# Decode attention: the first key block in one load, and TensorE starts when all of it has landed

## The chip, the cores and the metric

The kernel runs on one core of one Trainium2 chip. A core has TensorE (PE, with its weight loads shown as PEld), VectorE (DVE), ScalarE (ACT), GpSimd (POOL) and SyncE (SP). Each takes its instructions in program order, and they wait for each other through semaphores. Sixteen DMA engines move data between HBM and the on-chip memory. The metric is the device time of one execution in microseconds, the median of several runs.

## What is computed

One decoding step of grouped-query attention over a long cache, mixed by a gate with a small token-mixing network. The cache is nearly all of the data: 8 key/value heads of 65536 positions with 256 numbers each, in bfloat16, once for keys and once for values, 537 MB together.

```python
# x: [1, 1, 448]; k_cache, v_cache: [1, 8, 65536, 256]; wq: [448, 4096]; wo: [4096, 448]
q = (x @ wq).reshape(1, 1, 16, 256).transpose(0, 2, 1, 3)
k = repeat(k_cache, 2, axis=1); v = repeat(v_cache, 2, axis=1)
p = softmax(einsum("bhqd,bhkd->bhqk", q, k) * 256 ** -0.5)
a = einsum("bhqk,bhkd->bhqd", p, v).transpose(0, 2, 1, 3).reshape(1, 1, 4096) @ wo
h = layernorm(x)
b = (gelu(h[..., None] * w1 + b1) @ w2 + b2)        # a small network on each number of h
g = sigmoid((x * gate_w).sum())
out = g * a + (1 - g) * b
```

## The kernel before

**Blocks and chunks.** The keys are taken in `NP` = 32 blocks, four to a head, and the values likewise. A block is 16384 positions: `NV` = 128 slots of 128 positions by 256 numbers, 8.4 MB, 64 KB in each of 128 partitions. A block has `BODY` = 8 chunks of `NT` = 16 slots. `HV` = 64 slots are half a block, four chunks (`DC` = 4).

**The key ring.** `kring` has room for one and a half blocks, `NV + HV` slots. Blocks with an even number stand in slots 0 to 127, those with an odd number in slots 64 to 191. So the middle 64 slots are shared by each block and the next. TensorE takes the middle slots first (`tiles(HV)`, chunks 0 to 3), then the half that is a block's own (`tiles(0)` or `tiles(NV)`, chunks 4 to 7). Once chunks 0 to 3 are transposed the next block may be loaded. `vbuf` has room for one block of values; a new one may be loaded when TensorE has used the old one. At the start `vbuf` also holds the query weights `wq` and the small inputs.

**The order of loads.** All large loads are issued by SP in its program order, on one queue: `wo` for the first head, `wq`, key block 0 in two halves (L268 and L269), value block 0, key block 1, value block 1, key block 2, and so on. Ahead of each stands its wait: value block 0 waits for the query work that reads `vbuf` (`s_q`, `s_hb`), key block j for the transposes of chunk 3 of block j - 1 (`sem_tr`, L290), value block j for the products with value block j - 1 (`sem_pv`, L276). Key blocks 2, 3 and 31 also come in parts, each with semaphores of its own (`sem_kc`, `sem_kq`).

**TensorE's order.** After the query work a loop runs over the blocks. For block 0 and block 1: `keys` (for each chunk 16 transposes L355 into `kst`, which VectorE and ScalarE copy to `ktT` at L675 and L820, and 32 score products L376 one chunk behind), then the maxima (L393, L395) that VectorE turns into the softmax's shift, then `values` (denominators L400, then 128 products with the value block, L407, in pieces of 72, 24, 16 and 16). The last product tells `sem_pv`. From block 2 on the maxima and values of a block come after the keys of the next one.

**The waits around the change.** In `transposes`, chunk 0 of block j waits for `sem_k` to reach 16 (j + 1), and chunk 4 waits for `sem_kb` and, in three blocks, for one of `sem_kc`. The first half to be loaded of block 0, slots 64 to 127, counts on `sem_k`; the second one, slots 0 to 63, on `sem_kb`.

Of the kernel before, what the change touches and what calls it, by code (L numbers as in the profile page):

```python
# [12 lines left out]
def bass_gated_mix__gqa_block_cached__mixer_token_mlp__decode_kernel(  # L13
# [37 lines left out]
    NV = BODY * NT  # L51
# [32 lines left out]
    HV = NV // 2  # L84
# [11 lines left out]
    with ctx:  # L96
        def sb(shape, dt, name):
            return ctx.enter_context(nc.sbuf_tensor(name, shape, dt))
# [4 lines left out]
        def new_sem(name):  # L103
            return ctx.enter_context(nc.semaphore(name))

        kring = sb([P, NV + HV, DH], bf16, "kring")
# [87 lines left out]
        prj = psum([P, 512], f32, "prj")  # L194

        sem_k = new_sem("sem_k")
        sem_kb = new_sem("sem_kb")
        sem_kc = [new_sem("sem_kc%d" % i) for i in range(3)]
        sem_kq = [new_sem("sem_kq%d" % i) for i in range(2)]
        sem_v = new_sem("sem_v")  # L200
# [49 lines left out]
        def src(cache, j, n0=0, n1=NV):  # L250
            g, m = divmod(j, PPH)
            s = cache[0, g, m * BODY * CH:(m + 1) * BODY * CH, :].rearrange("(p n) d -> p n d", p=P)
            return s[:, n0:n1, :].rearrange("p n d -> p (n d)")

        @block.sync
        def _(eng):
            def load_wo(g):
                w = A_wo[g * REP * DH:(g + 1) * REP * DH, :]
                eng.dma_start(wo_rows, w.rearrange("(p i) n -> p (i n)", i=2 * REP)).then_inc(sem_wo, 16)

            load_wo(0)
            eng.dma_start(wq_s.rearrange("p u n -> p (u n)"),
                          A_wq.rearrange("r n -> (r n)").rearrange("(p m) -> p m", p=P)).then_inc(sem_wq, 16)
            def load(dst, cache, j, n0, n1, at, sem):
                eng.dma_start(dst[:, at + n0:at + n1, :].rearrange("p n d -> p (n d)"), src(cache, j, n0, n1)
                              ).then_inc(sem, 16)

            load(kring, A_k_cache, 0, HV, NV, 0, sem_k)  # L268
            load(kring, A_k_cache, 0, 0, HV, 0, sem_kb)  # L269

            def load_v(j):
                if j == 0:
                    eng.wait_ge(s_q, 1)
                    eng.wait_ge(s_hb, 1)
                else:
                    eng.wait_ge(sem_pv, j)  # L276
                load(vbuf, A_v_cache, j, 0, NV, 0, sem_v)
                g, m = divmod(j, PPH)
                if m == 0 and 1 <= g < H - 1:
                    eng.wait_ge(s_proj, g)  # L280
                    load_wo(g)

            for j in range(NP):
                if j == LEAD + 1:
                    eng.wait_ge(sem_tr[NB - 1], BODY * LEAD)
                    load(kring, A_k_cache, j, HV, NV, HV, sem_kc[1])
                    eng.wait_ge(sem_tr[NB - 1], BODY * LEAD + DC // 2)
                    load(kring, A_k_cache, j, 0, HV // 2, HV, sem_kq[0])
                if j >= 1:
                    eng.wait_ge(sem_tr[NB - 1], BODY * (j - 1) + DC)  # L290
                if j == LEAD:
                    load(kring, A_k_cache, j, HV, NV, 0, sem_k)
                    load(kring, A_k_cache, j, 0, HV, 0, sem_kc[0])
                elif j == LEAD + 1:
                    load(kring, A_k_cache, j, HV // 2, HV, HV, sem_kq[1])
                elif j == NP - 1:
                    load(kring, A_k_cache, j, 0, HV, HV, sem_k)
                    load(kring, A_k_cache, j, HV, NV, HV, sem_kc[2])
                elif j >= 1:
                    load(kring, A_k_cache, j, 0, NV, HV * (j % 2), sem_k)  # L300
                if j < LEAD:
                    load_v(j)
                elif j > LEAD:
                    load_v(j - 1)


            for (n0, n1), sem in zip(pieces, sem_vp):
                if n0 == 0:
                    eng.wait_ge(sem_tr[NB - 1], BODY * (NP - 1) + DC)
                elif n0 == NRING:  # L310
                    eng.wait_ge(sem_pv, NP - 1)
                load(kring if n1 <= NRING else vbuf, A_v_cache, NP - 1, n0, n1, 0, sem)
            eng.wait_ge(s_proj, H - 1)
            for h in range(REP):
                w = A_wo[(HQ - REP + h) * DH:(HQ - REP + h + 1) * DH, :]
                eng.dma_start(wo_sb[:, h, :], w.rearrange("(p j) n -> p (j n)", j=2)).then_inc(sem_wl[h], 16)
            eng.wait_ge(s_fin, NCG)
            eng.dma_start(out_ap, out_row[:, :]).then_inc(sem_out, 16)
            eng.wait_ge(sem_out, 16)
# [16 lines left out]
        def _(pe):  # L336
# [3 lines left out]
            def transposes(k, c, j, u16, x2):  # L340
                if k == 0:
                    pe.wait_ge(sem_k, u16)
                if k == DC:
                    pe.wait_ge(sem_kb, 16)
                    for p, sem in zip((LEAD, LEAD + 1, NP - 1), sem_kc):
                        with pe.If(j == p):
                            pe.wait_ge(sem, 16)

                done = pe.snap(c + 1, min_val=1, max_val=NC)

                def tiles(at):
                    for b in range(NB):
                        pe.wait_ge(sem_ev[b], done)
                        for i in range(4):
                            ins = pe.transpose(kst[:, b, i * P:(i + 1) * P],  # L355
                                               kring_f[:, at + NT * (k % DC) + 4 * b + i, :], ident[:, :])
                        ins.then_inc(sem_tr[b], 1)

                if k < DC:
                    tiles(HV)  # L360
                else:
                    with pe.If(x2 == 0):
                        tiles(0)
                    with pe.Else():
                        tiles(NV)
# [16 lines left out]
            def keys(c0, j, *where):  # L382
                j1 = pe.snap(j + 1, min_val=1, max_val=NP)
                transposes(0, c0, j, *where)
                for k in range(1, BODY):
                    transposes(k, c0 + k, j, *where)
                    scores(k - 1, c0 + k - 1, j1)
                scores(BODY - 1, c0 + BODY - 1, j1)
# [43 lines left out]
            def piece_wait(n):  # L432
                for (n0, _), sem in zip(pieces, sem_vp):
                    if n == n0:
                        pe.wait_ge(sem, 16)
# [423 lines left out]
```

## Time and profile before

| | |
|---|---|
| Median of 3 runs | 1264.3 us (1264.19 to 1264.69) |
| The profiled execution | 1264.2 us, span 1262.9 us |
| TensorE busy | 964.6 us, 76% of the span |
| VectorE, ScalarE busy | 500.2 us, 544.5 us |
| Mean granted clock of TensorE | 0.85 |
| DMA | 544.35 MB, mean 431 GB/s |

Times in the profile are counted from the start of the span. SPq is the queue of SP: it issues DMAs and has no busy time of its own. In the page's second part each digit is the busy share of a fortieth of the span, in tenths. In a timeline a row is: start, time taken, engine, line, operation, what it writes and reads, count, and in brackets how long the engine was idle before and what ended that. In the chain of what ended last a DMA row runs from issue to landing, and "issue" is time in which an engine waited for nothing that the profile shows. A DMA lands when the last of its sixteen parts has counted on its semaphore. In windows, the granted clock of TensorE, the DMA share and GB/s are the last three columns; a DMA packet is put down to the window in which it begins, so a share can be over 1.

### The profile page before, as it was taken

Reading aid. Unit: us, or ns where it says so; the run is one execution under the profiler, and the core shown is the slowest. Engines: PE = TensorE matmul, PEld = TensorE weight load, DVE = VectorE, ACT = ScalarE, POOL = GpSimd, SP = SyncE. Lnnn points to the kernel's source line nnn. Section 1 sums busy time; section 2 is a strip of 40 time slices with the busy share of each in tenths; the row PEclk is TensorE's granted clock in tenths of the full one; section 3 lists DMA queues with packets and bytes.
Section 4 is the critical chain, followed back from the end, with each engine's and each line's share of the span. In section 5 each row is a group of like instructions: output and inputs, shape, how many; then the busy total and the mean of one; then the engine's idle time right before and its main releaser. Section 6 shows DMA issues by size and latency. Waiting matters only on the chain.

```text
span 1262.9 us, 39617 instructions
## 1 busy us (share of the span) xinstructions
PE 964.6 (76%) x17024; PEld 881.7 (70%) x17024; DVE 500.2 (40%) x1128; ACT 544.5 (43%) x692; POOL 0.9 (0%) x7
## 2 busy tenths in 40 slices
PE   4768877688777797767878678876679867698786
PEld 3667876678766687666777667776678756687674
DVE  4334434444544435444444433343333423334342
ACT  2444543345533445333554334443344533345451
POOL 0000000000000000000000000000000000000000
PEclk8779887888878888888987879888798878888897
DMA  9999999999999999999999999999999999999998
GB/s 417 431 421 426 449 432 432 430 432 444 432 434 430 434 432 432 432 434 436 436 434 428 439 432 432 432 440 432 434 432 434 428 440 436 434 432 434 423 438 365
DMA packets 12053, 544.35 MB, mean 431 GB/s; under 512 B 1417, under 2 KB 1676, under 8 KB 2828
## 3 DMA queue, kind: packets, MB, share of 16 engines
q1 hardware_dynamic: 11954, 544.22, 99.7%
q8 instruction: 6, 0.10, 0.0%
q10 hardware_dynamic: 90, 0.01, 0.0%
q14 instruction: 3, 0.02, 0.0%
HBM read 544.22 MB, written 0.00 MB: 431 GB/s over the span
## 4 chain that ended last, share of the span: by engine, by line
DMA 60%; PE 36%; issue 2%; DVE 2%; DVEq 0%; ACT 0%; SPq 0%
DMA kring<-in_A_k_cache_dram 57%; PE kst L355 26%; PE sps L376 6%; DMA vbuf<-in_A_v_cache_dram 3%; PE acc L407 3%; PE acc L457 0%; PE prj L468 0%; PE sps L395 0%; DVE ktT L675 0%; DVE accs L709 0%; PE acc L400 0%; ACT z_b L825 0%; PE sps L393 0%; DVE mrow L686 0%; DVE z_b L656 0%
## 5 line engine op out<-in xcount | busy, mean ns | idle before, releaser
L355 PE MATMUL kst<-ident,kring 128*128 128x128 f32 x4096 | 556.9, 296 | 189.5 <-DMA kring<-in_A_k_cache_dram 166.6
L820 ACT ACTIVATE ktT<-kst 128x1024 bf16<-128x1024 bf16 x512 | 498.6, 1021 | 338.7 <-PE kst L355 338.3
L355 PEld LDWEIGHTS kst<-ident,kring 128*128 128x128 f32 x4096 | 505.1, 154 | 198.6 <-issue 192.3
L675 DVE COPY ktT<-kst 128x1024 bf16<-128x1024 bf16 x512 | 353.9, 692 | 436.0 <-PE kst L355 410.4
L376 PEld LDWEIGHTS sps<-qcur,ktT 128*128 128x128 bf16 x8192 | 238.0, 97 | 2.6
L376 PE MATMUL sps<-qcur,ktT 128*128 128x2 bf16 x8192 | 236.6, 163 | 0.0
L407 PE MATMUL acc<-vbuf,pT 128*2 128x256 bf16 x4008 | 160.0, 335 | 6.5 <-DMA vbuf<-in_A_v_cache_dram 3.7
L407 PEld LDWEIGHTS acc<-vbuf,pT 128*2 128x2 bf16 x4008 | 110.8, 102 | 47.6 <-issue 4.4
L803 ACT ACTIVATE fade<-mdif 128x2 f32<-128x2 f32 x32 | 6.5, 203 | 302.1 <-DVE mdif L692 302.1
L686 DVE TENSOR_REDUCE mrow<-sps 2x1 f32<-2x128 f32 x32 | 8.9, 278 | 159.9 <-PE sps L393 159.9
L395 PEld LDWEIGHTS sps<-mdiag,mones 2*128 2x128 f32 x64 | 11.2, 217 | 28.0 <-DVE mdiag L688 28.0
L807 ACT ACTIVATE pT<-sps,mneg 128x64 f32 x128 | 30.4, 335 | 0.0
L395 PE MATMUL sps<-mdiag,mones 2*128 2x2 f32 x64 | 13.9, 285 | 21.3 <-DVE mdiag L688 21.3
L393 PE MATMUL sps<-ident,mcol 128*2 128x128 f32 x32 | 9.0, 282 | 27.3 <-issue 25.8
L825 ACT ACTIVATE z_b<-z_b 128x448 bf16<-128x448 bf16 x14 | 8.1, 576 | 48.1 <-DVE z_b L662 48.1
L400 PE MATMUL acc<-pT,ones_sq 128*128 128x32 bf16 x256 | 12.0, 182 | 21.9 <-issue 18.4
L709 DVE COPY accs<-acc 128x288 f32<-128x288 f32 x8 | 3.7, 458 | 62.4 <-PE acc L407 62.4
L393 PEld LDWEIGHTS sps<-ident,mcol 128*2 128x2 f32 x32 | 2.6, 80 | 36.2 <-issue 28.1
L681 DVE TENSOR_REDUCE mcol<-sps 128x2 f32<-128x256 f32 x32 | 13.5, 423 | 33.8 <-PE sps L376 33.8
L400 PEld LDWEIGHTS acc<-pT,ones_sq 128*128 128x128 bf16 x256 | 8.8, 99 | 26.0 <-issue 22.3
L704 DVE TENSOR_SCALAR acc<-acc,fader 128x256 f32<-128x256 f32 x32 | 15.8, 493 | 2.5
L497 PE MATMUL kst<-vbuf,xcol 128*64 128x512 bf16 x28 | 5.5, 571 | 8.8 <-DMA vbuf<-in_A_wq_dram 8.8
(111 smaller groups left out, 173.9 us busy)
## 6 DMA issues: line engine op xcount, KB each, us to landing
kring<-in_A_k_cache_dram SPq DMA_DIRECT2D x7, 4096.0 KB, 26.4
kring<-in_A_v_cache_dram SPq DMA_DIRECT2D x1, 4608.0 KB, 27.6
kring<-in_A_k_cache_dram SPq DMA_DIRECT2D x2, 2048.0 KB, 15.1
vbuf<-in_A_wq_dram SPq DMA_DIRECT2D x1, 3584.0 KB, 12.0
wo_sb<-in_A_wo_dram SPq DMA_DIRECT2D x7, 448.0 KB, 25.5
vbuf<-in_A_v_cache_dram SPq DMA_DIRECT2D x1, 1536.0 KB, 9.3
vbuf<-in_A_v_cache_dram SPq DMA_DIRECT2D x1, 1024.0 KB, 11.4
vbuf<-in_A_v_cache_dram SPq DMA_DIRECT2D x1, 768.0 KB, 12.8
```

The source lines that it names most:

```text
L355: ins = pe.transpose(kst[:, b, i * P:(i + 1) * P], kring_f[:, at + NT * (k % DC) + 4 * b + i, :], ident[:, :])
L376: ins = pe.matmul(sps[:, 0, 2 * (NT * k + nt):2 * (NT * k + nt) + 2], ktT[:, par, b, ntl * DH + dj:(ntl + 1) * DH:2], qcur[:, dj, :], star ...
L393: pe.transpose(mxT, mcol[:, :], ident[:, :]).then_inc(s_mT, 1)
L395: pe.matmul(mxB, mones[:, :], mdiag[:, :], start=True, stop=True).then_inc(s_mB, 1)
L400: pe.matmul(acc[:, DENC:SELC], ones_sq[:, :], pT[:, r, :], start=False, stop=(r == BODY - 1), skip_group_check=True)
L407: ins = pe.matmul(acc[o:o + REP, 0:DH], pT[:, r, 2 * nt:2 * nt + 2], buf[:, n, :], start=False, stop=False, skip_group_check=True)
L675: vec.tensor_copy(ktT[:, k % KTB, b, :], kst_b[:, b, :]).then_inc(sem_ev[b], 1)
L681: vec.tensor_reduce(out=mcol[:, :], in_=scores_all.rearrange("p (n hh) -> p hh n", hh=REP), axis=AX.X, op=ALU.max)
L686: vec.tensor_reduce(out=mrow[:, :], in_=mxT, axis=AX.X, op=ALU.max)
L704: vec.tensor_scalar(acc[:, 0:DENC], acc[:, 0:DENC], fader[:, :], None, op0=ALU.mult).then_inc(s_acc, 1)
L807: ins = act.activation(pT[:, bass.ds(p0, DC), hh:2 * NT:REP], scores_all.rearrange("p (a r n hh) -> p a hh r n", a=2, r=DC, hh=REP)[:, hal ...
L820: act.activation(ktT[:, k % KTB, b, :], kst_b[:, b, :], AF.Copy).then_inc(sem_ev[b], 1)
```

## The change

Key block 0 is loaded by one DMA of 128 slots that counts on `sem_k`. The semaphore `sem_kb` and the wait for it before chunk 4 are gone. As `sem_k` now reaches 16 only with the whole block, chunk 0 waits for all of it.

```diff
-        sem_kb = new_sem("sem_kb")
...
-            load(kring, A_k_cache, 0, HV, NV, 0, sem_k)
-            load(kring, A_k_cache, 0, 0, HV, 0, sem_kb)
+            load(kring, A_k_cache, 0, 0, NV, 0, sem_k)
...
                 if k == 0:
                     pe.wait_ge(sem_k, u16)
                 if k == DC:
-                    pe.wait_ge(sem_kb, 16)
                     for p, sem in zip((LEAD, LEAD + 1, NP - 1), sem_kc):
```

The kernel after has three lines less, so what stood at L265, L355, L376 and L407 stands at L264, L352, L373 and L404.

SP's first rows before, with their waits. Rows of L265 are the loads of keys and values, and the two sizes a partition's numbers in half a block (16384) and in a whole one (32768); `sem_tr3` is the last of the four `sem_tr`:

```order
L259 DMA wo_sb<-in_A_wo_dram 128x1792
L262 DMA vbuf<-in_A_wq_dram 128x14336
L265 DMA kring<-in_A_k_cache_dram 128x16384 x2
L265 DMA vbuf<-in_A_v_cache_dram 128x32768 [waits s_hb,s_q]
L265 DMA kring<-in_A_k_cache_dram 128x32768 [waits sem_tr3]
L265 DMA vbuf<-in_A_v_cache_dram 128x32768 [waits sem_pv]
```

And after:

```order
L258 DMA wo_sb<-in_A_wo_dram 128x1792
L261 DMA vbuf<-in_A_wq_dram 128x14336
L264 DMA kring<-in_A_k_cache_dram 128x32768
L264 DMA vbuf<-in_A_v_cache_dram 128x32768 [waits s_hb,s_q]
L264 DMA kring<-in_A_k_cache_dram 128x32768 [waits sem_tr3]
L264 DMA vbuf<-in_A_v_cache_dram 128x32768 [waits sem_pv]
```

Two half loads became one whole load at the same place, and the rows behind it stand as they did.

TensorE's rows before chunk 4, before the change. The scores of chunk 2 end here, then come the branches for the blocks that load in parts:

```order
L376 MATMUL sps<-qcur,ktT 128x2 x32
L346 COMPARE_AND_BRANCH [waits sem_kb]
L346 UNCONDITIONAL_BRANCH [waits sem_kc0]
L346 COMPARE_AND_BRANCH
L346 UNCONDITIONAL_BRANCH [waits sem_kc1]
```

And after:

```order
L373 MATMUL sps<-qcur,ktT 128x2 x32
L343 COMPARE_AND_BRANCH
L343 UNCONDITIONAL_BRANCH [waits sem_kc0]
L343 COMPARE_AND_BRANCH
L343 UNCONDITIONAL_BRANCH [waits sem_kc1]
```

Only the wait went; no instruction of TensorE moved.

## The prediction

> **What bounds the kernel now.** I read the page first, then what the loads on the SP queue wait for, then the chain and the timeline of the first 130 us, because the change touches one load near the start.
>
> ```profile
> PE 964.6 (76%) x17024; PEld 881.7 (70%) x17024; DVE 500.2 (40%) x1128; ACT 544.5 (43%) x692; POOL 0.9 (0%) x7
> ...
> DMA  9999999999999999999999999999999999999998
> ...
> q1 hardware_dynamic: 11954, 544.22, 99.7%
> q8 instruction: 6, 0.10, 0.0%
> ```
>
> The SP loads' queue (q1) fills 99.7% of sixteen DMA engines' time, TensorE 76%. The 544 MB set the time, as long as the next load is always queued before the one ahead of it drains. So the one question is whether the change lets the queue run dry, and for how long: a dry microsecond is not made up, since no later slice is idle.
>
> ```profile
> SPq L265 <- PE kst L355: 610.2, 34, 26.9
> SPq L265 <- PE acc L407: 569.0, 30, 28.3
> ```
>
> These are the waits of the SP queue itself. Key loads wait for transposes (L355), value loads for the value products (L407). A late TensorE therefore makes loads late, and the lead of each load over the landing of the one ahead of it is the slack. The issues near the start, and two of the steady part, are these (2.13 and 83.42 are each the second of a pair, shown by a narrower window):
>
> ```profile
> 0.74 0.40 SPq L259 DMA_DIRECT2D wo_sb<-in_A_wo_dram  x1
> ...
> 2.13 0.43 SPq L265 DMA_DIRECT2D kring<-in_A_k_cache_dram  x1
> 21.76 0.33 SPq L265 DMA_DIRECT2D vbuf<-in_A_v_cache_dram  x1
> 34.79 0.33 SPq L265 DMA_DIRECT2D kring<-in_A_k_cache_dram  x1
> 63.44 0.33 SPq L265 DMA_DIRECT2D vbuf<-in_A_v_cache_dram  x1
> 83.05 0.82 SPq L265 DMA_DIRECT2D kring<-in_A_k_cache_dram  x2
> ...
> 83.42 0.45 SPq L265 DMA_DIRECT2D kring<-in_A_k_cache_dram  x1
> ...
> 143.41 0.33 SPq L265 DMA_DIRECT2D kring<-in_A_k_cache_dram  x1
> 162.67 0.33 SPq L265 DMA_DIRECT2D vbuf<-in_A_v_cache_dram  x1
> ```
>
> The time from issue to landing comes last in each row of the list of DMA issues, asked for one issue at a time. In order: the very first load (wo, issued at 0.74), the second half of key block 0 (2.13), value block 0 (21.76), value block 1 (63.44), the two halves of key block 2 (83.05 and 83.42), key block 4 (143.41), value block 3 (162.67).
>
> ```profile
> wo_sb<-in_A_wo_dram SPq DMA_DIRECT2D x1, 448.0 KB, 3.4
> ...
> kring<-in_A_k_cache_dram SPq DMA_DIRECT2D x1, 4096.0 KB, 31.2
> ...
> vbuf<-in_A_v_cache_dram SPq DMA_DIRECT2D x1, 31.4
> ...
> vbuf<-in_A_v_cache_dram SPq DMA_DIRECT2D x1, 28.2
> ...
> kring<-in_A_k_cache_dram SPq DMA_DIRECT2D x1, 4096.0 KB, 18.3
> ...
> kring<-in_A_k_cache_dram SPq DMA_DIRECT2D x1, 4096.0 KB, 27.7
> ...
> kring<-in_A_k_cache_dram SPq DMA_DIRECT2D x1, 25.9
> ...
> vbuf<-in_A_v_cache_dram SPq DMA_DIRECT2D x1, 26.0
> ```
>
> So the second key half lands at 33.3, value block 0 at 53.2 and value block 1 at 91.6. Value block 3 is issued 6.6 us before key block 4 lands (143.4 + 25.9 = 169.3).
>
> The chain that ended last, in its first 75 us, then TensorE's own timeline:
>
> ```profile
> 1.66 21.21 DMA kring<-in_A_k_cache_dram
> 22.87 0.92 issue
> 23.79 5.80 PE kst L355 x32
> ...
> 34.79 37.53 DMA kring<-in_A_k_cache_dram
> 72.32 0.13 issue
> 72.46 5.40 PE kst L355 x32
> ```
>
> ```profile
> 53.18 4.43 PE L407 MATMUL acc<-vbuf,pT 128*2 128x256 bf16 x77 [0.65 <-DMA vbuf<-in_A_v_cache_dram]
> 60.46 2.94 PE L407 MATMUL acc<-vbuf,pT 128*2 128x256 bf16 x51 [2.85 <-issue]
> ```
>
> The first key half lands at 22.87 and TensorE starts at 23.79. The 0.92 is not the load: TensorE was still walking into its loop, since at 72.32 the same wait costs 0.13. Key block 1 lands at 72.32. Value block 1 is issued at 63.44, when the products end at 60.46 + 2.94 = 63.40. Its lead is 72.32 - 63.44 = 8.9 us.
>
> **The change part by part.**
>
> *One load in place of two.* Two halves of a block land 9.7 us apart (83.42 + 27.7 less 83.05 + 18.3, about 9.75). A whole load takes 91.6 - 72.3 = 19.3. Two halves are thus 0.1 to 0.2 us dearer than a whole. SP issues one DMA less at 2.1 us, hidden, as nothing on SP follows before 21.76. The block's landing is the next item's. I count 0 for the transfer; the bounds are -0.2 and 0.
>
> *The wait before chunk 4 goes.* The second half had landed at 33.3, before key block 1's release at 34.79 and chunk 4 behind it. It held nothing up: 0.
>
> *TensorE's start moves.* The whole block lands at 22.9 + 9.7 = 32.6 at the earliest and at 33.3, as the second half did, at the latest; I take 33.0, the middle. With 0.13 TensorE starts at 33.1 in place of 23.79: 9.3 us later. Behind this wait stand, on TensorE, all transposes and scores of block 0, then its maxima and value products. VectorE, ScalarE and SP wait for those.
>
> *Key block 1.* Its issue goes from 34.79 to 44.1. Value block 0, ahead of it in the queue, lands at 53.2 as before, since its issue at 21.76 waits for the query work and not for keys. The lead falls from 18.4 to 9.1 us: 0.
>
> *Value block 1.* The products now start with value block 0 long landed, so the 0.65 wait at 53.18 falls away, and they end 9.3 - 0.65 = 8.65 later. The issue goes from 63.44 to 72.1. The lead of 8.9 is eaten but for 0.2 us, and a load cannot start at once. This is where the change costs.
>
> *The restart of an empty queue.* No load of before meets an empty queue but the first, and these rows bound what it adds:
>
> ```profile
> 0.70:1.70 1.00, 0.00 (x0) 0.00 (x0) 0.54 (x1) 0.00 (x0) 0.58 (x3) 1.00 0.01 1
> 1.70:1.90 0.20, 0.00 (x0) 0.00 (x0) 0.20 (x1) 0.00 (x0) 0.12 (x1) 1.00 0.92 143
> ...
> SPq L319 <- DMA out_dram<-out_row: 0.8, 1, 0.8
> ```
>
> The last two columns of the windows are DMA share and GB/s: nothing moves until about 1.0 us after the issue at 0.74. That first load lands after 3.4 us, of which 448 KB at a whole block's rate (8192 KB in 19.3 us) are 1.1, so 2.3 are overhead. It meets the program's start, so this is the upper bound. The output's 0.9 KB needs 0.8 us of waiting after an issue of 0.3: 1.1 in all, the lower bound. I take 1.7, the middle.
>
> By the Trainium skill, "DMA: Bandwidth & Descriptors", Specifications, the first byte on this path comes after about 0.6 us; the 1.0 above is longer, and by the page's figure the forecast would be 0.4 us lower. The trace's row is used.
>
> *The sum.* Value block 1 lands at 72.1 + 1.7 + 19.3 = 93.1 in place of 91.6: 1.5 us later. To that I add 0.2, because a code block that is loaded once behind the first products (the last of six on q8, shown below) falls after the restart and takes from one engine's time; its bounds are 0 and 0.7 (0.10 MB in six is 17 KB each; an engine moves 512 KB of a block in 19.3 us, 27 KB in 1 us).
>
> *After that.* Key block 2's first half was issued 83.05 - 72.46 = 10.6 after TensorE began block 1. It now begins at about 72.6, the issue falls at 83.2, and value block 1 lands at 93.1: a lead of 9.9. From there every wait of TensorE is for a landing, and all leads are as before, 6.6 us or more. So 1.7 us is passed on whole to the end: 1264.2 (the profiled execution's own time, span 1262.9) + 1.7 = 1265.9. The median of the three runs, 1264.3, is 0.1 higher, within their spread.
>
> *What may move the issue at 72.1.* The clock of TensorE is half when it starts, as it was before:
>
> ```profile
> 24.70:28.10 3.40, 3.40 (x17) 3.40 (x17) 1.38 (x2) 1.63 (x2) 0.00 (x0) 0.50 1.07 451
> 28.10:31.50 3.40, 3.40 (x57) 3.39 (x57) 1.91 (x3) 2.46 (x4) 0.00 (x0) 1.00 1.20 520
> ...
> 55.40:58.80 3.40, 2.20 (x41) 1.08 (x30) 0.00 (x0) 0.00 (x0) 0.00 (x0) 0.50 1.18 506
> ...
> L407 PE MATMUL acc<-vbuf,pT 128*2 128x256 bf16 x128 | 5.2, 339 | 0.0
> ...
> q8 instruction: 1, 0.02, 1.6%
> ...
> q8 instruction: 1, 0.02, 1.4%
> ```
>
> The third column from the end is the granted clock: 0.50, full from 28.1, and 0.50 again in the products. The next row is the products of value block 1 (from 100 us on): 5.2 us against 10.2 for block 0, which ran at half clock with the 2.85 stall inside. From TensorE's start to the issue that its fourth chunk releases block 0 took 11.0 us (23.79 to 34.79), block 1 10.6 (72.46 to 83.05). I allow 0.5 either way for where the clock steps up. The 2.85 is the other term: "issue" with no releaser, in the first pass only. The last two rows are the code loads by DMA from 57 to 61 us and from 63 to 68 us, one each; the first stands beside the stall. I keep the stall, as the same first pass runs.
>
> The Trainium skill, "Runtime: NRT & Kernel Launch", Instruction fetch mechanics, says that a taken branch to a page outside a two-page window forces a fetch before execution goes on. The 2.85 behind the branch to the last products agrees; that the second pass has 0.0 idle does not. By the rule the stall stays, as in the sum.
>
> **The rivals.**
>
> *The transfer is hidden anyway.* If the 2.85 stall shrinks to nothing, because TensorE's code comes in while it waits for the keys, value block 1 is issued at 69.2, 3.1 us before key block 1 lands. That is more than the restart, and the time is 1264.2. Against it: the code that is missing lies behind 77 of the 128 products, and TensorE stands at its loop's head while it waits for keys.
>
> *Slower by more than can be overlooked.* One mechanism: an empty queue restarts slowly. At the upper bound, 2.3, and the issue 0.5 late at 72.6, value block 1 lands at 94.2, 2.6 us later, and the time is 1266.8 or more. It decides from a restart of 2.7 at the issue of 72.1. For it speaks the 3.4 of the first load; against it that this load met the start.
>
> *The whole delay arrives.* 9.3 us at the end, 1273.5. It needs key block 1 to be late; its lead of 9.1 speaks against it.
>
> *A gain.* If each load paid its overhead also in a full queue, one load less would give 2.3 us: 1261.9. The 0.1 to 0.2 between two halves and a whole speaks against it. The Trainium skill, "DMA: Bandwidth & Descriptors", Anatomy of one DMA, puts about 2.0 us fixed on each DMA of another issuing path; an estimate by that page is 1262.2, and this trace, where loads follow without a gap, does not agree.
>
> **How the numbers follow.** The short dry stretch, 0.5 to 2.5 us, has 0.57; hidden, 0.14; slower by the slow restart, 0.23; the whole delay, 0.03; a gain, 0.03. A measurement here tells about 0.2%, 2.5 us, from no change. So faster is 0.03, same 0.57 + 0.14 = 0.71, slower 0.23 + 0.03 = 0.26. The prediction is 1265.9. The bounds together, an issue at 71.5 to 72.8 (the landing and the clock not both at their ends) and a restart of 1.1 to 2.3, then 0 to 0.7, give +0.3 to +3.5; with the hidden case below and a little of the slow one above the range is 1264.0 to 1267.9, which leaves the last two rivals and the tail of the slow one out.
>
> **What would show it.** Right: TensorE's first transpose at 33.1, key block 1 issued near 44 with no dip in DMA, no wait ahead of the first value products, value block 1 issued near 72, one window around 73 with a DMA share well under 1, and all later issues shifted by one and the same 1.5 to 2 us. Wrong: value block 1 issued before 70 (hidden), a second dip near 93, or a dip of more than 2.5 us.

## The result and the profile after

| | before | after |
|---|---|---|
| Median | 1264.35 us (6 runs, 1264.09 to 1264.69) | 1268.1 us (6 runs, 1267.41 to 1270.26) |
| Profiled execution | 1264.2 us, span 1262.9 | 1267.4 us, span 1266.1 |
| Ratio | | 1.0034, 95% interval 1.0023 to 1.0045 |

The kernel became slower by 3.75 us at the median, 0.30%; the ratio in the table, which is not that of the medians, says 0.34%. The profiled execution is the fastest of the six, 3.2 us over its counterpart. The runs now spread over 2.9 us where those of before spread over 0.6 (54 later runs of the kernel before: 1263.8 to 1266.2, all but one below 1265.4).

The page of the kernel after, DMA share and rate in fortieths of the span, and the queue of the SP loads:

```profile
DMA  9989999999999999999999999999999999999998
GB/s 424 428 361 431 446 431 431 445 431 431 431 431 445 431 431 431 431 445 431 431 431 431 445 431 431 431 443 433 431 431 431 443 433 431 431 431 431 431 431 379
...
q1 hardware_dynamic: 11810, 544.22, 99.5%
```

One slice, the third (63 to 95 us), lost its 9; all others stand. What happened is inside it. SP's issues:

```profile
1.66 0.42 SPq L264 DMA_DIRECT2D kring<-in_A_k_cache_dram  x1
21.13 0.33 SPq L264 DMA_DIRECT2D vbuf<-in_A_v_cache_dram  x1
44.22 0.33 SPq L264 DMA_DIRECT2D kring<-in_A_k_cache_dram  x1
72.88 0.33 SPq L264 DMA_DIRECT2D vbuf<-in_A_v_cache_dram  x1
84.74 33.38 SPq L264 DMA_DIRECT2D kring<-in_A_k_cache_dram  x5
...
145.70 0.33 SPq L264 DMA_DIRECT2D kring<-in_A_k_cache_dram  x1
```

The time from issue to landing of key block 1 and of value block 1, in the list of DMA issues:

```profile
kring<-in_A_k_cache_dram SPq DMA_DIRECT2D x1, 27.9
...
vbuf<-in_A_v_cache_dram SPq DMA_DIRECT2D x1, 21.8
```

Key block 1 lands at 44.2 + 27.9 = 72.1, as before (72.3). Value block 1 is issued 0.7 us behind that, 9.4 later than before, and lands at 72.88 + 21.8 = 94.7 in place of 63.44 + 28.2 = 91.6: 3.0 late. The windows around it (granted clock, DMA share and GB/s last) show the queue dry:

```profile
68.00:70.00 2.00, 0.10 (x4) 0.10 (x8) 0.00 (x0) 0.00 (x0) 0.00 (x0) 0.52 0.62 262
70.00:72.00 2.00, 2.00 (x44) 1.26 (x40) 0.00 (x0) 0.00 (x0) 0.00 (x0) 0.50 0.04 8
72.00:73.00 1.00, 0.83 (x15) 0.26 (x7) 0.00 (x0) 0.00 (x0) 0.00 (x0) 0.50 0.00 0
73.00:74.00 1.00, 0.51 (x3) 0.52 (x4) 0.00 (x0) 0.00 (x0) 0.00 (x0) 0.50 0.97 328
```

From 70 to 73 almost no packet begins. What was begun before 70 still runs for a while: by the packets' own times in the trace no load moves on any of the sixteen engines from 71.7 to 73.8, for 2.1 us. TensorE's own rows:

```profile
33.39 5.63 PE L352 MATMUL kst<-ident,kring 128*128 128x128 f32 x32 [11.74 <-DMA kring<-in_A_k_cache_dram]
62.15 3.56 PE L404 MATMUL acc<-vbuf,pT 128*2 128x256 bf16 x77
69.89 2.94 PE L404 MATMUL acc<-vbuf,pT 128*2 128x256 bf16 x51 [4.18 <-issue]
73.49 6.05 PE L352 MATMUL kst<-ident,kring 128*128 128x128 f32 x32 [0.65 <-issue]
```

It starts 9.6 us later, waits for no values any more, and its stall inside the products is 4.18 in place of 2.85. The idle time ahead of block 1's transposes shrank to 0.65. Before, it was a wait of 9.06 for key block 1:

```profile
72.46 5.40 PE L355 MATMUL kst<-ident,kring 128*128 128x128 f32 x32 [9.06 <-DMA kring<-in_A_k_cache_dram]
```

### The profile page after: what moved, and what is told of

It is laid out like the page before. It is cut to its first block, busy times and chain, and to the rows that moved or that the text cites. A ratio compares the mean times of both kernels' runs of the same rounds, so it can differ in the third digit from the quotient of the medians.

```text
span 1266.1 us, 39616 instructions
## 1 busy us (share of the span) xinstructions
PE 976.4 (77%) x17024; PEld 893.3 (71%) x17024; DVE 500.2 (40%) x1128; ACT 546.1 (43%) x692; POOL 0.9 (0%) x7
## 4 chain that ended last, share of the span: by engine, by line
DMA 58%; PE 38%; issue 2%; DVE 2%; DVEq 0%; SPq 0%; ACT 0%
DMA kring<-in_A_k_cache_dram 55%; PE kst L352 27%; PE sps L373 6%; PE acc L404 3%; DMA vbuf<-in_A_v_cache_dram 2%; DMA wo_sb<-in_A_wo_dram 1%; PE acc L454 0%; PE sps L392 0%; PE prj L465 0%; PE acc L397 0%; DVE ktT L672 0%; PE sps L390 0%; ACT z_b L822 0%; DVE mrow L683 0%; SPq L264 0%
## 5 line engine op out<-in xcount | busy, mean ns | idle before, releaser
L352 PE MATMUL kst<-ident,kring 128*128 128x128 f32 x4096 | 565.9, 299 | 182.3 <-DMA kring<-in_A_k_cache_dram 159.9
L352 PEld LDWEIGHTS kst<-ident,kring 128*128 128x128 f32 x4096 | 514.1, 156 | 191.4 <-issue 186.3
L373 PEld LDWEIGHTS sps<-qcur,ktT 128*128 128x128 bf16 x8192 | 238.0, 97 | 2.6
L373 PE MATMUL sps<-qcur,ktT 128*128 128x2 bf16 x8192 | 236.6, 163 | 0.0
L404 PE MATMUL acc<-vbuf,pT 128*2 128x256 bf16 x4008 | 164.2, 341 | 5.1 <-issue 4.2
L404 PEld LDWEIGHTS acc<-vbuf,pT 128*2 128x2 bf16 x4008 | 113.7, 104 | 47.2 <-issue 5.2
L392 PEld LDWEIGHTS sps<-mdiag,mones 2*128 2x128 f32 x64 | 11.0, 213 | 27.9 <-DVE mdiag L685 27.9
```

Of the source, the lines that this page charges most:

```text
L352: ins = pe.transpose(kst[:, b, i * P:(i + 1) * P], kring_f[:, at + NT * (k % DC) + 4 * b + i, :], ident[:, :])
L373: ins = pe.matmul(sps[:, 0, 2 * (NT * k + nt):2 * (NT * k + nt) + 2], ktT[:, par, b, ntl * DH + dj:(ntl + 1) * DH:2], qcur[:, dj, :], star ...
L392: pe.matmul(mxB, mones[:, :], mdiag[:, :], start=True, stop=True).then_inc(s_mB, 1)
L404: ins = pe.matmul(acc[o:o + REP, 0:DH], pT[:, r, 2 * nt:2 * nt + 2], buf[:, n, :], start=False, stop=False, skip_group_check=True)
```

## The experiments

Theory A: TensorE's late start makes value block 1 late, its lead is used up, and the queue of loads runs dry once. The rivals stand with each run. Times are medians beside the runs of the kernel before on the same chip (1264.15 to 1264.3), with the ratio to it and its 95% interval.

**Late start without the whole load** (`late_two_halves`), from the kernel before:

```diff
                 if k == 0:
                     pe.wait_ge(sem_k, u16)
+                    pe.wait_ge(sem_kb, 16)
                 if k == DC:
-                    pe.wait_ge(sem_kb, 16)
```

> The two half loads of the kernel before stay; only TensorE's wait for the second half moves from chunk 4 to chunk 0 (the late start without the whole load). Theory A (the late start makes value block 1 late, its queue runs dry once): first transpose near 33.4, value block 1 issued at 72 to 74.5, time 1267.4 to 1270.3, as the changed kernel. Rival B (the form of the load, one DMA of 64 KB per partition in place of two of 32 KB, is what costs): 1264.3, as before.

1268.34 us, 1.0035 (1.0021 to 1.0049): all of the change's cost without the whole load. Rival B is out. In its profile (TensorE's first transposes, the stall, value block 1's issue and its time to landing):

```profile
33.66 5.85 PE L355 MATMUL kst<-ident,kring 128*128 128x128 f32 x32 [11.66 <-DMA kring<-in_A_k_cache_dram]
...
70.67 2.94 PE L407 MATMUL acc<-vbuf,pT 128*2 128x256 bf16 x52 [4.55 <-issue]
...
73.65 0.33 SPq L265 DMA_DIRECT2D vbuf<-in_A_v_cache_dram  x1
...
vbuf<-in_A_v_cache_dram SPq DMA_DIRECT2D x1, 21.9
```

**The changed kernel once more** (`after_again`, no edit):

> The changed kernel once more, for a second profile: the six times were 1267.4 to 1270.3, a spread of 2.9 us where the kernel before has 0.6. Theory A: the span's excess over 1262.9 equals, within 0.4 us, the lateness of value block 1's landing against 91.6, and that lateness follows from its issue (issue + 19.3 + about 2.5); the scatter is that of TensorE's first pass (code stall in the first products, clock). Rival E (scatter from somewhere else, such as HBM speed): landing of value block 1 as in the first profile, and the rest late.

1267.92 us (1267.4 to 1270.5), 1.0032 (1.0020 to 1.0045).

```profile
70.14 2.94 PE L404 MATMUL acc<-vbuf,pT 128*2 128x256 bf16 x51 [3.94 <-issue]
...
73.12 0.33 SPq L264 DMA_DIRECT2D vbuf<-in_A_v_cache_dram  x1
...
vbuf<-in_A_v_cache_dram SPq DMA_DIRECT2D x1, 21.9
```

Value block 1 lands at 95.0, 3.4 late, and the span is 1266.8, 3.9 over before. In the first profile it was 3.0 and 3.2, in the run above (95.5) 3.9 and 4.4. So the lateness of that landing is the excess of the span to within 0.5 us; the 0.4 named ahead holds in one of the three. In these three the lateness follows the issue, 72.9 to 73.7. The slowest executions, 1270.2 to 1271.1, have no profile, so for them this is not shown.

**The restart by itself** (`restart_26`), from the kernel before:

```diff
                     eng.wait_ge(sem_pv, j)
+                if 4 <= j <= 29:
+                    eng.wait_ge(sem_k, 16 * (j + 2))
                 load(vbuf, A_v_cache, j, 0, NV, 0, sem_v)
```

> The kernel before, with one more wait: 26 value loads (blocks 4 to 29) are issued only when the key block ahead of them has landed, so each meets an empty queue. This measures the restart by itself. With the 2.5 us that the changed kernel's profile shows (94.7 - 72.9 - 19.3): 26 x 2.5 = 65, and 0.1 each for SP to see the landing: 1329 to 1333. With the 1.7 of the prediction: 1309 to 1312. TensorE's other slack (24 us of transposes in a 41 us period) should hide the rest.

1331.3 us in one run: (1331.3 - 1264.15) / 26 = 2.58 us for each empty queue. The median time to landing of its value loads (31, of which 26 met an empty queue), and the windows around one that was issued at 208.34, its key block having landed at 208.3:

```profile
vbuf<-in_A_v_cache_dram SPq DMA_DIRECT2D x31, 21.9
...
208.00:209.00 1.00, 0.60 (x3) 0.61 (x4) 0.78 (x3) 0.00 (x0) 0.00 (x0) 0.50 0.00 0
209.00:210.00 1.00, 1.00 (x7) 1.00 (x6) 0.84 (x3) 0.00 (x0) 0.00 (x0) 0.50 3.10 1049
```

21.9 from issue to landing is 2.6 more than the 19.3 of a load behind another, and the same as in the changed kernel. The restart of an empty queue costs 2.6 us here. The changed kernel's trace shows two parts of it: the first packet begins 0.96 us after the issue (73.84), and the first packets of the sixteen engines take 2.5 to 3.4 us each, where the later ones take 2.42.

**A smaller delay** (`first_96`, `first_112`), from the kernel before, with 32 (or 16) in place of `HV`:

```diff
-            load(kring, A_k_cache, 0, HV, NV, 0, sem_k)
-            load(kring, A_k_cache, 0, 0, HV, 0, sem_kb)
+            load(kring, A_k_cache, 0, 32, NV, 0, sem_k)
+            load(kring, A_k_cache, 0, 0, 32, 0, sem_kb)
```

> Key block 0 in two loads again, but the first has 96 slots (the four chunks that TensorE takes first, and 32 slots more), the second 32. TensorE starts some 4 us later than before, at about 27.8. Theory A: value block 1 is issued near 67 (66 to 68.5), a lead of 4 us or more over key block 1's landing, which hides the restart: 1264.3, within 0.3. Rival C (any delay of TensorE's start is passed on in proportion, 3.75 us for 9.6): +1.6, 1265.9.

> The same with 112 slots first and 16 after. TensorE starts at about 30.3, value block 1 is issued near 69.7 (68.7 to 71.3), a lead of about 2.5. The slowest DMA engine ends key block 1 some 0.5 before the landing, and the first bytes come 1.0 to 1.8 after an issue. Theory A: 0 to 0.9 more than before, 1264.3 to 1265.2. Rival C: +2.5, 1266.8.

1265.42 us (1264.3 to 1266.0), 1.0006 (0.9996 to 1.0016), and 1266.61 us (1265.4 to 1268.1), 1.0018 (1.0009 to 1.0028). Both lie between the theories, nearer to rival C's numbers than to mine, and the first one's interval takes in no change at all. The profile of `first_96`, TensorE and SP:

```profile
28.76 6.55 PE L355 MATMUL kst<-ident,kring 128*128 128x128 f32 x32 [6.92 <-DMA kring<-in_A_k_cache_dram]
...
53.28 0.55 PE L355 MATMUL kst<-ident,kring 128*128 128x128 f32 x3 [2.15 <-issue]
...
67.86 2.94 PE L407 MATMUL acc<-vbuf,pT 128*2 128x256 bf16 x51 [3.59 <-issue]
...
70.84 0.33 SPq L265 DMA_DIRECT2D vbuf<-in_A_v_cache_dram  x1
```

The issue came at 70.84, not near 67: the start was 5.0 us late in place of 4, the first 32 transposes took 6.55 against 5.80 at a lower granted clock (0.54 against 0.62), a stall of 2.15 stands inside chunk 7 (0.49 before), and one of 3.59 in the products (2.85 before). Key block 1 landed at 72.2, so the lead was 1.4; a restart of 2.6 leaves 1.2 of it unhidden, and value block 1 landed 1.1 late, at 92.7. The mechanism holds, and my size for the delay did not.

In `first_112` the issue came at 69.75, as expected, but key block 1 itself landed 1.3 us late, at 73.6, and value block 1 at 93.7, 2.0 late. By the trace fifteen of key block 1's sixteen parts had landed by 72.1. The last one's engine, its packets put in order by their starts and ends, carried a load of program code in between (64.36 to 65.43), and its next data packet ended 1.5 us later than it would have otherwise. Value block 1's last part came by another engine, whose first packet began 3.0 us after the issue; why it began so late is not settled.

**A larger delay** (`start_v0`), from the changed kernel:

```diff
                 if k == 0:
                     pe.wait_ge(sem_k, u16)
+                    pe.wait_ge(sem_v, 16)
```

> The changed kernel, but TensorE's first transposes also wait for value block 0, so they start at 53.2, 29.4 us later than before in place of 9.6. Theory A (beyond the lead every microsecond counts, and each dry queue restarts in 21.9 us from issue to landing): key block 1 issued at 64, landed at 86; value block 1 issued at 92.6, landed at 114.5, 22.9 later than before: 1286 to 1289. Rival C (the same share of the delay as in the changed kernel, 3.75 of 9.6): 1276.

1285.81 us (1285.2 to 1286.4), 1.0170 (1.0153 to 1.0187). That is just below the 1286 expected at least, as value block 1 was issued at 90.6 and not at 92.6; rival C's 1276 is out. Against the changed kernel TensorE starts 52.89 - 33.39 = 19.5 later and the time is 17.7 longer. The difference is the stall, which is shorter here:

```profile
87.65 2.90 PE L405 MATMUL acc<-vbuf,pT 128*2 128x256 bf16 x52 [2.09 <-issue]
...
90.60 0.33 SPq L264 DMA_DIRECT2D vbuf<-in_A_v_cache_dram  x1
```

19.5 - (4.18 - 2.09) = 17.4. Beyond the lead, each microsecond of TensorE is one of time. The queue was running out while this stall ran (85.6 to 87.7), as key block 1 landed at 63.44 + 23.1 = 86.5. Of the profiled execution's excess over before (22.0) 20.7 stand at value block 1's landing, 112.3; the rest comes behind 1007 us, where one more code load runs.

**The code in one piece** (`straight_code` from the changed kernel, `straight_before` from the kernel before; the last block's version of the products and `tail` go behind, into the second branch):

```diff
-                    some(0, NRING, vbuf)
+                    some(0, NLATE, vbuf).then_inc(s_early, 1)
+                    some(NLATE, NV, vbuf).then_inc(sem_pv, 1)
                 with pe.Else():
                     piece_wait(0)
                     some(0, NRING, kring)
...
```

> The changed kernel with the code of the value products written in another order: all 128 products of an ordinary block stand in one piece, and the last block's own version behind them, so the first pass takes no branch among the products. The same products in the same order. Theory A with the code stall as its term (4.2 us in the changed kernel's profile): without the stall value block 1 is issued near 68.7, a lead of 3.4, and the restart is hidden: 1264.2 to 1264.8. Rival F (the stall is not tied to the branch and comes back elsewhere ahead of the last product): issue at 72 to 74, 1267 to 1270.

> The kernel before with the value products' code in one piece, as in the run straight_code: a control for what that order of the code costs by itself. Theory A: value block 1 still issued 6 us or more before key block 1 lands, so 1264.1 to 1264.5. If the order of the code itself costs (more code, loaded later): 1265 to 1266, by a delay that shows at key block 2 or 4.

1265.13 us (1264.4 to 1267.4), 1.0009 (1.0000 to 1.0019): 0.3 over the range expected, with four of ten executions inside it. The control: 1264.23 us, 0.9999 (0.9990 to 1.0009). In the profile of `straight_code` (an execution of 1266.9):

```profile
58.18 0.55 PE L352 MATMUL kst<-ident,kring 128*128 128x128 f32 x3 [2.06 <-issue]
...
64.74 6.29 PE L404 MATMUL acc<-vbuf,pT 128*2 128x256 bf16 x128
...
71.08 0.33 SPq L264 DMA_DIRECT2D vbuf<-in_A_v_cache_dram  x1
...
76.51 5.60 PE L352 MATMUL kst<-ident,kring 128*128 128x128 f32 x32 [5.47 <-issue]
```

The 128 products now run without a break, and the median is 2.8 us nearer to before: the stall was a term of the cost. The edit takes the branch out and moves the code behind it at the same time, so which of the two removed the stall is not shown. The other stalls grew, as rival F had it in part: 2.06 in chunk 7 (0.76 in the changed kernel), which put the issue at 71.08 and not near 68.7, and 5.47 behind the products (0.65), where SP no longer waits. The control shows that this order costs nothing while there is a lead.

**Value block 1 earlier** (`early_v1`), from the changed kernel; `s_part` counts the 72nd product:

```diff
...
+                    if j == 1:
+                        eng.wait_ge(s_part, 1)
+                        load(vbuf, A_v_cache, j, 0, NRING, 0, sem_v)
                     eng.wait_ge(sem_pv, j)
-                load(vbuf, A_v_cache, j, 0, NV, 0, sem_v)
+                if j == 1:
+                    load(vbuf, A_v_cache, j, NRING, NV, 0, sem_v1)
+                else:
+                    load(vbuf, A_v_cache, j, 0, NV, 0, sem_v)
...
-                    some(0, NRING, vbuf)
+                    some(0, NRING, vbuf).then_inc(s_part, 1)
+                    with pe.If(j == 1):
+                        pe.wait_ge(sem_v1, 16)
```

> The changed kernel (one whole load, late start), but value block 1 comes in two loads: slots 0 to 71 as soon as the first 72 products with value block 0 are done, the other 56 slots after all of them. TensorE is as late as in the changed kernel. Theory A: the first part is issued near 66.5, before key block 1 has drained, the queue never runs dry, 1264.2 to 1264.6. Rival D (TensorE's late start itself, its maxima and products, goes to the end): 1267.4 to 1270.3.

1268.89 us (1267.3 to 1271.4), 1.0042 (1.0025 to 1.0059): what I expected did not come. The profile says where it went (SP's issues, TensorE's start of block 1, DMA windows):

```profile
66.46 7.31 SPq L266 DMA_DIRECT2D vbuf<-in_A_v_cache_dram  x2
88.69 33.13 SPq L266 DMA_DIRECT2D kring<-in_A_k_cache_dram  x5
...
149.34 0.33 SPq L266 DMA_DIRECT2D kring<-in_A_k_cache_dram  x1
...
77.97 5.51 PE L360 MATMUL kst<-ident,kring 128*128 128x128 f32 x32 [4.57 <-issue]
...
72.00:74.00 2.00, 1.40 (x28) 0.60 (x20) 0.00 (x0) 0.00 (x0) 0.00 (x0) 0.50 0.74 313
...
148.00:150.00 2.00, 2.00 (x45) 1.99 (x42) 1.39 (x2) 1.47 (x2) 0.00 (x0) 1.00 0.00 0
```

The dry stretch near 72 is gone. But TensorE stalled 4.57 us behind the products and was 5.5 us late in block 1; nothing between gave that back, key block 4 was issued at 149.34 in place of 143.41, and the queue ran dry there. The delay was turned into a wait of another load: key block 4 landed at 171.3 in place of 169.3, which is 2.0 of this execution's 3.1 us. The rest comes behind 832 us, where one more code load runs.

**The same without the new branch** (`early_v1_pool`): the `pe.If` is dropped, both parts have semaphores of their own, and GpSimd passes them on.

```diff
...
+            for sem in sem_v1:
+                eng.wait_ge(sem, 16)
+            eng.sem_inc(sem_v, 16)
             for sem in sem_kq:
...
```

> The changed kernel with value block 1 in two loads again, the first 72 slots released after 72 products; but GpSimd collects the two landings, so TensorE's code has no branch and no wait more than the changed kernel. TensorE stays some 9.6 us late. Theory A, with the second limit that the run before showed (key block 4's issue, which had come 5.9 us later than in the kernel before, and too late): value block 1's first part issued near 66, no dry stretch near 73; key block 2 issued near 85 and key block 4 near 145.7, before value block 2 lands at 150: 1264.2 to 1265.0. Rival D (the late start goes to the end whatever load is moved): 1267.4 to 1270.3, with a dry stretch near 148.

1265.79 us (1264.0 to 1267.2), 1.0011 (1.0001 to 1.0020): over the range of theory A and under that of rival D. Three of ten executions are at 1264.0 to 1264.3, which rival D does not allow; nothing in the edit starts TensorE earlier, though no profile shows these three. The others are between. The profile is of one of 1267.1, near the top (SP's issues of value block 1 and key block 4, and the latter's time to landing, stand last):

```profile
58.02 0.55 PE L363 MATMUL kst<-ident,kring 128*128 128x128 f32 x3 [2.22 <-issue]
...
68.63 7.27 SPq L266 DMA_DIRECT2D vbuf<-in_A_v_cache_dram  x2
...
147.74 0.33 SPq L266 DMA_DIRECT2D kring<-in_A_k_cache_dram  x1
...
kring<-in_A_k_cache_dram SPq DMA_DIRECT2D x1, 24.4
```

There the first part came at 68.6, 2.2 later than in `early_v1` (66.46): 1.2 by the stall in chunk 7 (2.22 against 1.05) and 0.9 by the first 32 transposes (6.57 against 5.63). No dry stretch stands near 73 (DMA shares of 0.88 and 1.04 from 70 to 74). But key block 4 landed at 147.74 + 24.4 = 172.1 in place of 169.3, and these 2.8 us are nearly all of the execution's excess (span 1265.8 against 1262.9). It was issued 3.3 us ahead of value block 2's landing (151.05), and this lead did not hide the restart: fifteen of its sixteen parts had landed by 170.5, the last came by an engine that began 3.3 us after the issue. So in this execution the delay did go on to another load, near the place that rival D names. No version was found that beats the kernel before, whose queue is never dry.

## Why the prediction was right or wrong

**Right, in its mechanism.** The page's 99.7%, the wait that SP's value load has on TensorE, the lead of 8.9 us and its being used up are what the profile after shows: the first transposes at 33.4 (said: 33.1), key block 1 at 44.2 (44.1) with its lead, no wait for value block 0, and one dry stretch near 72. The later issues are not shifted by one and the same 1.5 to 2 us, as the sign had it, but by 1.7 (84.74) to 2.4 (165.03). That the halves or the whole make no difference `late_two_halves` confirms. That the wait before chunk 4 cost nothing the idle time ahead of it shows, 0.48 us with the wait and without it:

```profile
36.02 1.96 PE L355 MATMUL kst<-ident,kring 128*128 128x128 f32 x16 [0.48 <-issue]
...
45.45 1.96 PE L352 MATMUL kst<-ident,kring 128*128 128x128 f32 x16 [0.48 <-issue]
```

The whole 9.6 did not arrive, and no gain came.

**Wrong, in two sizes.** The time was put at 1265.9, with 1267.9 at the top; it is 1268.1. What I ranked as less likely, slower by more than 0.2%, came, and by its mechanism.

First, the step "The restart of an empty queue": 1.7 us, as the middle of 1.1 and 2.3. It is 2.5 in the profile after (72.88 to 94.7, less 19.3) and 2.58 on average over 26. It lies over my upper bound too. That bound came from the first load with a transfer of 1.1 us taken off; and a middle between a 0.9 KB store and a load was no estimate for an 8 MB load, to which the load's row was the nearer one. The Trainium skill, "DMA: Bandwidth & Descriptors", Anatomy of one DMA, has about 2.0 us fixed for a DMA on another issuing path; the 2.58 here is longer, and it is paid only where the queue is empty.

Second, the step "Value block 1": an issue at 72.1. It came at 72.9, 73.1 and 73.7 in three profiles with the full delay. The start was 0.3 to 0.6 later than taken, and the stall in the products, which I carried over as 2.85, was 4.18, 3.94 and 4.55. A faster granted clock in the first 77 products (0.65 in place of 0.50) gave some back: 3.56 in place of 4.43 us. The prediction kept this stall as a constant. It is none: 2.09 to 4.55 in ten profiles with nearly the same code, among them 3.38 in `restart_26`, whose first pass is that of the kernel before.

What it waits for stands in the traces. In all ten the stall ends 1.3 to 1.5 us behind the end of a 16 KB load of program code (q8; in the changed kernel the load runs from 67.69 to 68.61 and the stall to 69.89). Each of these ten loads starts where a 64 KB data packet ends, and such a packet takes 2.42 us. If the code is asked for at any moment within a packet, this alone scatters the stall by 2.4 us; that it is the scatter is argued, not shown. The Trainium skill, "Runtime: NRT & Kernel Launch", Instruction fetch mechanics, says that a taken branch to code that is not at hand forces a fetch by DMA. The runs agree as far as they go: the stall stands beside a code load, and in one piece the products had none; but it comes behind the 76th or 77th product, and the branch stands behind the 72nd.

Together: 1.5 of the sum's lateness became 3.0 to 3.9.

**The 0.2 for a code block after the restart** was not there: in the profile after, the last of the six code loads begins at 71.05, in the dry stretch. The upper bound of 0.7 was too small as well, as the 1.5 in `first_112` shows.

**"From there every wait of TensorE is for a landing"** is not so: block 2's transposes wait for no landing (1.35 of "issue" before, at 106.60, and 1.40 after, at 108.76). They follow TensorE's own work, so lateness in block 1 goes on to key block 4, as `early_v1` showed. In the change as made the leads were long enough for it (key block 2 at 84.74, 10.0 ahead of value block 1's landing; key block 4 at 145.70, 7.3 ahead of value block 2's at 153.0).

**Open.** Why one engine in `first_112` and one in `early_v1_pool` began a load only 3.0 and 3.3 us after its issue; and what share of the scatter of 2.9 us is the stalls' and what the clock's, as each profile shows only one execution.

## What to carry to other kernels

Where the DMA queue is full all the time, list for each load how long ahead of the last landing it is issued, and measure a delay against the smallest of these leads. A delay was free here only while what was left of the lead held the restart; beyond that every microsecond was paid. Leads of 1.4 and 3.3 us were not enough (`first_96`, `early_v1_pool`), one of 2.6 was (value block 3 of `early_v1`), and so were all of 5 us and more. A landing is that of the last of sixteen engines, and the first of them can be through 1.9 us earlier (key block 1 of the changed kernel: 70.3 to 72.1), so a lead counted from the landing is kinder than what the first engine has. Stalls that are hidden today, as in the first pass through a loop, become part of the time and of its scatter once the lead is gone.

## What the runs showed of the hardware that I had not expected

An empty queue's restart costs 2.58 us for an 8 MB load, measured over 26 of them in one execution. TensorE's stalls in the first pass through its loop differ from execution to execution of nearly the same code: 0.22 to 2.22 us in chunk 7, 2.09 to 4.55 in the products, 0.65 to 5.47 behind them. Those in the products end 1.3 to 1.5 us behind a code load. A 16 KB code load puts the data of its engine back by 1.5 us (`first_112`).
